# Retention attention, routing and experts in one kernel: the attention's products put in another order on TensorE

## The chip, the cores and the metric

The kernel runs on one core of a Trainium2 chip. The metric is the time of one execution on the device, in microseconds (us), as the median of several executions. The engines are PE (TensorE, the matmuls; PEld is its weight load), DVE (VectorE), ACT (ScalarE), POOL (GpSimd) and SP (SyncE, which here issues most transfers). Each has its own instruction stream, which it works through in order.

## The reference

Three layers follow one another, all in float32. In the attention, each head keeps a state that decays by a fixed factor at every position; eight heads of 64, two batches of 768 positions:

```python
for t in range(S):
    state = gamma * state + einsum('bhd,bhe->bhde', k[:, :, t], v[:, :, t])
    y[:, :, t] = scale * einsum('bhd,bhde->bhe', q[:, :, t], state)
x = y as 1536 rows of 512
# experts: two of eight per row, by noisy logits
noisy = x @ w_gate + log1p(exp(x @ w_noise)) * noise
top2, weights = the two largest, softmax over the two
out[rows of e] += weight * (relu(x[rows of e] @ w1[e]) @ w2[e])
# last layer
h = out @ w_in;  solu = h * softmax(h)
out = layer_norm(solu) * g_ln @ w_out
```

## The kernel before

**Tiles.** The attention works on 12 tiles of 128 positions: six chunks c of each of two batches b, in the order (c, b). The heads stand in pairs. For tile i these are the steps; the lines are those of the kernel before.

- `scores(i)`: 8 matmuls that use half of the array's rows each (L432) write queries times keys into a bank; DVE multiplies by the causal mask (L436). The result is PM(i).
- `y_out(i)`: 4 matmuls on the full array bring queries times state ("state(i)", L445; none for the first chunk), and 8 on half of the array's columns add PM(i) times the scaled values ("values(i)", L449), into the one bank `c2`. DVE copies this, scaled, to XT(i) (L452) and so frees the bank.
- `kv(i)`: 4 matmuls on the full array add keys times values to the state ("keys(i)", L460; none in the last chunk). ACT copies the result to S (L466).
- `x_rows(i)`: 4 matmuls on the full array turn XT(i) into rows, with the routing's logits beside them (L482). ACT copies the two halves to x (L485, L487), DVE copies the logits to lgs and adds the second half (L486, L488), SP stores x.
- `scale_v(i)`: the values scaled by the decay, vp(i), on DVE for i < 5 and from there in 8 instructions on ACT (L422). `dec_t` makes the decay tables decT in 4 instructions on ACT (L301).
- `feed`: loads units of the experts' weights (wr, L182, SP) and splits each into a high part wh on ACT (L200) and a low part wl on DVE (L201). The wl of a unit waits in the list `later` and is written down at the next tile's place for it.

In fp32r, the form that the experts' matmuls use, a value is a sum of two parts; hence `wh`, `wl` and `xh`, `xl`.

**Routing.** It goes by four groups of tiles, g = 0 to 3, of 4, 4, 2 and 2 tiles. `choose(g)` is a generator: two functions on ACT (L504, L505), a chain of 11 small instructions on DVE (L507 to L513), then the two largest logits, `chosen` and `cum` (L517 to L520), then their indices (L523). `rank(g)` counts on PE (L533), with ACT's copy rks (L534); `first_rows(g)` makes `s` (L544) and compares `col`, the column numbers, with it to a one-hot `oh` (L548). `list_part` multiplies `oh` on PE (L607, L613) to lists of rows (L619), by which POOL gathers rows of x (L622); `first_xt` transposes these (L635) for the first expert. `slots`, `add_table` and `by_rows` (L565 to L601) make the table of places. `hidden(0, f)` is the first expert's first layer (L724).

**What sets the order.** One loop over i, written by hand, sets the order of all these on each engine. Before the change, tile i runs state(i) and values(i), then keys(i), then scores(i+1), then x(i), and the routing's pieces stand between by conditions on i. PE changes between half rows, half columns and the full array four times per tile from the third tile on. The first expert's weights follow: `feed` loads the units (whose number is `LEAD` and a few) during the tiles. After the attention come the experts 0 to 7, which PE paces, then the last layer and the stores (L958, L959).

## Time and profile before

| what | value |
|---|---|
| three executions | 517.97, 518.2, 519.29 us; median 518.2 |
| the profiled execution | 519.29 us |
| its span in the profile | 517.6 us |
| PE clock granted | 0.999 |
| PE, PEld, DVE, ACT, POOL busy | 98, 89, 71, 45, 19% |

The profile is of one execution. Its span goes from the first to the last recorded instruction; the execution's own time is 1.7 us longer. A busy share is an average over stages that have different limits: the attention is the first 72 us of the span, the experts and the last layer the rest.

### The profile page before, as it was taken

Reading aid. Unit: us, or ns where it says so; the run is one execution under the profiler, and the core shown is the slowest. Engines: PE = TensorE matmul, PEld = TensorE weight load, DVE = VectorE, ACT = ScalarE, POOL = GpSimd, SP = SyncE. Lnnn points to the kernel's source line nnn. Section 1 sums busy time; section 2 is a strip of 40 time slices with the busy share of each in tenths; the row PEclk is TensorE's granted clock in tenths of the full one; section 3 lists DMA queues with packets and bytes.
Section 4 is the critical chain, followed back from the end, with each engine's and each line's share of the span. In section 5 each row is a group of like instructions: output and inputs, shape, how many; then the busy total and the mean of one; then the engine's idle time right before and its main releaser. Section 6 shows DMA issues by size and latency. Waiting matters only on the chain.

```text
span 517.6 us, 8642 instructions
## 1 busy us (share of the span) xinstructions
PE 506.3 (98%) x3068; PEld 462.9 (89%) x3068; DVE 370.1 (71%) x750; ACT 233.5 (45%) x435; POOL 98.4 (19%) x202
## 2 busy tenths in 40 slices
PE   8999999999999999999999999999999999999996
PEld 7888888989999999999999999998878788888886
DVE  4769888747776976878778778799277668566650
ACT  2487642544344443344435443445254544444431
POOL 4000011431201203103003000002244346411120
PEclk9999999999999999999999999999999999999999
DMA  8999531498999988979999967567553565653341
GB/s 253 310 403 317 194 114 42 145 318 277 292 309 267 292 249 215 335 209 262 319 236 315 290 203 240 192 182 211 158 187 89 176 184 142 204 142 103 101 123 46
DMA packets 71857, 111.92 MB, mean 216 GB/s; under 512 B 9760, under 2 KB 37152, under 8 KB 71808
## 3 DMA queue, kind: packets, MB, share of 16 engines
q1 hardware_dynamic: 65520, 94.58, 60.5%
q0 software_dynamic: 4944, 16.39, 9.7%
q8 instruction: 26, 0.43, 0.3%
q10 hardware_dynamic: 1344, 0.34, 0.3%
q14 instruction: 23, 0.19, 0.1%
HBM read 83.50 MB, written 27.79 MB: 215 GB/s over the span
## 4 chain that ended last, share of the span: by engine, by line
PE 74%; DVE 13%; issue 6%; DMA 3%; ACT 2%; POOL 0%; SPq 0%; POOLq 0%; DVEq 0%; ACTq 0%
PE c L1068 18%; PE b L952 12%; PE b L724 11%; PE a L724 10%; PE d L865 10%; PE c L1190 3%; PE s L432 2%; DVE wl L201 2%; PE c L449 2%; DMA wr<-in_moe_w_dram 2%; PE c L460 1%; DVE pm L436 1%; PE c L445 1%; DVE rt L510 1%; PE c L482 1%
## 5 line engine op out<-in xcount | busy, mean ns | idle before, releaser
L201 DVE TENSOR_TENSOR wl<-wr,wh 128x1024 fp32r<-128x1024 f32 x68 | 81.5, 1218 | 14.5 <-issue 7.8
L1068 PE MATMUL c<-hh,wh 128*128 128x448 f32 (+5 forms) x224 | 78.9, 352 | 0.0
L1068 PE MATMUL c<-hh,wl 128*128 128x448 f32 (+5 forms) x224 | 78.8, 352 | 0.0
L1068 PE MATMUL c<-hl,wh 128*128 128x448 f32 (+5 forms) x224 | 78.8, 352 | 0.0
L200 ACT ACTIVATE wh<-wr 128x1024 fp32r<-128x1024 f32 x68 | 69.5, 1049 | 8.7 <-DMA wr<-in_moe_w_dram 8.7
L724 PE MATMUL b<-xh,wh 128*128 128x192 f32 (+8 forms) x144 | 47.1, 335 | 0.3 <-ACT xh L639 0.3
L724 PE MATMUL b<-xh,wl 128*128 128x192 f32 (+8 forms) x144 | 46.6, 331 | 0.0
L1068 PEld LDWEIGHTS c<-hh,wh 128*128 128x128 f32 x224 | 42.1, 188 | 1.1
L1068 PEld LDWEIGHTS c<-hh,wl 128*128 128x128 f32 x224 | 42.0, 188 | 1.1
L1068 PEld LDWEIGHTS c<-hl,wh 128*128 128x128 f32 x224 | 42.1, 188 | 1.1
L724 PE MATMUL a<-xh,wh 128*128 128x256 f32 (+7 forms) x128 | 43.0, 340 | 0.0
L724 PE MATMUL a<-xh,wl 128*128 128x256 f32 (+7 forms) x128 | 42.8, 339 | 0.0
L952 PE MATMUL b<-wh,zh 128*128 128x512 f32 (+1 forms) x104 | 38.5, 376 | 0.6 <-ACT zh L941 0.6
L865 PE MATMUL d<-wh,x2h 128*128 128x512 f32 x96 | 38.8, 404 | 0.0
L952 PE MATMUL b<-wl,zh 128*128 128x512 f32 (+1 forms) x104 | 38.4, 375 | 0.0
L865 PE MATMUL d<-wl,x2h 128*128 128x512 f32 x96 | 37.9, 395 | 0.0
L865 PE MATMUL d<-wh,x2l 128*128 128x512 f32 x96 | 37.8, 394 | 0.0
L728 ACT ACTIVATE hh<-b 128x192 fp32r<-128x192 f32 (+8 forms) x36 | 17.1, 476 | 43.6 <-PE b L724 40.6
L728 ACT ACTIVATE hh<-a 128x256 fp32r<-128x256 f32 (+7 forms) x32 | 15.9, 497 | 45.3 <-PE a L724 45.3
L1105 POOL COPY pace<-hh 1x1 f32<-1x1 f32 x20 | 8.7, 437 | 133.3 <-ACT hh L728 79.1
L1031 ACT ACTIVATE xh<-xt 128x428 fp32r<-128x428 f32 (+5 forms) x24 | 13.0, 540 | 44.8 <-DVE xt L1029 44.8
L878 ACT ACTIVATE ee<-d,st 128x1024 f32<-128x1024 f32 x12 | 13.4, 1117 | 41.7 <-DVE st L871 41.7
(259 smaller groups left out, 1100.4 us busy)
## 6 DMA issues: line engine op xcount, KB each, us to landing
wr<-in_moe_w_dram SPq DMA_DIRECT2D x60, 512.0 KB
zd<-zs SPq DMA_DIRECT2D x40, 128.0 KB
zc<-zd SPq DMA_DIRECT2D x10, 512.0 KB
xs<-xr SPq DMA_DIRECT2D x18, 256.0 KB
raw<-in_moe_w_in_dram SPq DMA_DIRECT2D x8, 512.0 KB
raw<-in_moe_w_out_dram SPq DMA_DIRECT2D x8, 512.0 KB
xq<-xs SPq DMA_DIRECT2D x16, 208.0 KB
yg<-yr SPq DMA_DIRECT2D x16, 208.0 KB
```

What stands on the lines that cost most here:

```text
L200: nc.scalar.activation(hi, t, AF.Copy)
L201: low = lambda: nc.vector.tensor_sub(lo, t, hi)
L432: nc.tensor.matmul(p[:, s, hp, :], KT[i][r, hp, :], QT[i][r, hp, :], start=True, stop=True)
L449: nc.tensor.matmul(py[s * 64:s * 64 + 64, hp, :], VP[i][:, 2 * hp + s, :], PM[i][hp // 2][:, hp % 2, s, :], start=(not c), stop=True, skip ...
L724: nc.tensor.matmul(p, w[:, 0, f * 128:(f + 1) * 128], x[:, d, c], start=(n == 0), stop=(n == len(terms) - 1))
L728: nc.scalar.activation(hh[:, f, c], p, AF.Relu)
L865: nc.tensor.matmul(PH[i][:, s, :], x[:, c], w[:, 0, f], start=(n == 0), stop=(n == 3 * KD - 1))
L878: nc.scalar.activation(ee, ph, AF.Exp, bias=col(0), accum_out=col(1))
L952: nc.tensor.matmul(p, z[:, f * 128:(f + 1) * 128], unit_t[8 * E + 4 + f // 2][n][:, f % 2, c], start=(m == 0), stop=(m == len(terms) - 1))
L1031: nc.scalar.activation(hi, t, AF.Copy)
L1068: nc.tensor.matmul(py[d][:, :CAPS[e]], c, h[:, f, :CAPS[e]], start=(f == 0 and n == 0), stop=(f == KF - 1 and n == 2))
L1190: nc.tensor.matmul(py, h[:, f, c], w[:, f % 2], start=(f == 0 and n == 0), stop=(f == KF - 1 and n == 2))
```

## The change

Keys(i), state(i) and x(i-1), all on the full array, now stand together, then values(i), then scores(i+1). `y_out` is cut into `from_state` and `y_out`. The routing's pieces move with this to other places in the loop; rank(2) and first_rows(2) move from the end of the attention to behind the first `hidden(0, 0)`. The column numbers `col` become F16. `feed` splits the first unit one tile earlier and loads the third and the fourth one tile later, and low parts that wait in `later` are not written down at tile 4. The second half of the last store is issued by ACT. Lines of the new kernel stand 4 higher from L453 on.

```diff
-    col = rt.tile([128, CAPS[0]], F32, name="col", bufs=1)
+    col = rt.tile([128, CAPS[0]], F16, name="col", bufs=1)
...
-    def y_out(i):
+    def from_state(i):
         c, b = order[i]
-        py = bank("c2", (128, HP, 128))
+        py = PO[i] = bank("c2", (128, HP, 128))
         if c:
             for hp in range(HP):
                 nc.tensor.matmul(py[:, hp, :], S_bufs[b, c % 2][:, hp, :], QT[i][:, hp, :],
                                  start=(hp == 0), stop=False, skip_group_check=True)
+
+    def y_out(i):
+        c, b = order[i]
+        py = PO.pop(i)
...
     for i in range(NT):
         load_qk(i + 3)
         load_kv(i + 3)
-        if i == 0:
-            kv(i)
+        kv(i)
+        from_state(i)
+        if i:
+            x_rows(i - 1)
+        if i == 6:
+            rank(0)
+            next(picks, None)
+        if i == 10:
+            list_part(0, range(4, 8), "a", last=True)
+            next(picks, None)
+        if i in (4, 8, 10):
+            picks = choose((4, 8, 10).index(i))
+            next(picks)
         y_out(i)
-        if i in (5, 8, 11):
+        if i in (5, 8):
             next(picks)
         if i == 7:
             next(todo, None)
-        if i:
-            kv(i)
+        if i == NT - 1:
+            for d in (0, 2):
+                first_xt(0, d, f"c{d // 2}")
+            next(picks)
+        scores(i + 1)
+        if i in (4, 8, 10):
+            next(picks)
         if i == 8:
             add_table(0)
             by_rows()
         if i == 9:
             rank(1)
             first_rows(1)
-        if i == NT - 1:
-            for d in (0, 2):
-                first_xt(0, d, f"c{d // 2}")
-            rank(2)
-        scores(i + 1)
-        if i in (4, 8, 10):
-            next(picks)
-        if i == 9:
-            next(picks, None)
...
-        for low in later:
-            low()
-        later = []
+        if i != 4:
+            for low in later:
+                low()
+            later = []
...
-        x_rows(i)
-        if i == 5:
-            rank(0)
-            next(picks, None)
-        if i == 9:
-            list_part(0, range(4, 8), "a", last=True)
-        if i in (3, 7, 9, 11):
-            if i == NT - 1:
-                last_picks = picks
-            picks = choose((3, 7, 9, 11).index(i))
-            next(picks)
         scale_v(i + 2)
         if i % 2 == 0:
             dec_t(i // 2 + 1)
-        feed(min(max(i - 2, 0), LEAD), min(i, LEAD + 3), later)
-    next(picks)
-    next(picks)
-    first_rows(2)
-    guard(EARLY_TILES)
+        feed((0, 0, 1, 1, 2, 3)[i] if i < 6 else LEAD, (0, 1, 2, 2, 3)[i] if i < 5 else min(i, LEAD + 3), later)
+    x_rows(NT - 1)
+    last_picks = picks
+    picks = choose(3)
+    for _ in range(3):
+        next(picks)
...
-        nc.sync.dma_start(out[row0(i):row0(i) + 128, c], o[:, c])
+        (nc.scalar if c.stop == DM and c.start else nc.sync).dma_start(out[row0(i):row0(i) + 128, c], o[:, c])
...
-    def newest():
-        rank(3)
-        first_rows(3)
+    def newest(g):
+        rank(g)
+        first_rows(g)
+        if g == 2:
+            guard(EARLY_TILES)
...
-        hidden(0, f, slice(0, EARLY), newest if f == 2 else None)
+        hidden(0, f, slice(0, EARLY), (lambda: newest(2 + f // 2)) if f in (0, 2) else None)
```

The instruction lists of both kernels show three places. A row has the line, the operation, the tile written and those read, and the shape; numbers behind a name tell buffers apart.

On PE, tile 4 before, from x(3), which writes `c_535`, to x(4), which writes `c_619`:

```order
L482 MATMUL c_535<-unit_166,xT 128x144 x2
L482 MATMUL a<-unit_167,xT 128x144 x2
L445 MATMUL c_572<-qt,S_227 128x128 x4
L449 MATMUL c_572<-pm,vp 64x128 x8
L460 MATMUL c_254<-vp,kn 128x128 x4
L432 MATMUL s<-qt,kt 128x128 x8
L482 MATMUL c_619<-unit_166,xT 128x144 x2
L482 MATMUL a<-unit_167,xT 128x144 x2
```

The same place after, from values(3) to scores(5):

```order
L453 MATMUL c_498<-pm,vp 64x128 x8
L432 MATMUL s<-qt,kt 128x128 x8
L464 MATMUL c_254<-vp,kn 128x128 x4
L445 MATMUL c_562<-qt,S_227 128x128 x4
L486 MATMUL c_567<-unit_166,xT 128x144 x2
L486 MATMUL a<-unit_167,xT 128x144 x2
L453 MATMUL c_562<-pm,vp 64x128 x8
L432 MATMUL s<-qt,kt 128x128 x8
```

Here x(3), which is `c_567`, moved from ahead of state(4) to behind it, keys(4) moved from behind values(4) to ahead of state(4), and scores(5) follow the values at once.

On ACT, before, from the state copy of tile 4 (`S_229`) to that of tile 5 (`S_233`); x<-c_619 is x(4):

```order
L466 ACTIVATE S_229<-c_254 64x4x64 x2
L485 ACTIVATE x<-c_619 128x256
L487 ACTIVATE x<-a 128x256
L422 ACTIVATE vp<-vt,dec 128x64 x8
L301 ACTIVATE decT<-decT,step 128x128 x4
L200 ACTIVATE wh<-wr 128x1024
L466 ACTIVATE S_233<-c_255 64x4x64 x2
```

After, from the same state copy; x<-c_567 is x(3) and x<-c_655 is x(4):

```order
L470 ACTIVATE S_229<-c_254 64x4x64 x2
L489 ACTIVATE x<-c_567 128x256
L491 ACTIVATE x<-a 128x256
L508 ACTIVATE rt<-lgs 128x32
L509 ACTIVATE rt<-lgs 128x32
L422 ACTIVATE vp<-vt,dec 128x64 x8
L301 ACTIVATE decT<-decT,step 128x128 x4
L200 ACTIVATE wh<-wr 128x1024
L470 ACTIVATE S_233<-c_255 64x4x64 x2
L489 ACTIVATE x<-c_655 128x256
L491 ACTIVATE x<-a 128x256
```

x(4) stood ahead of the scaled values vp(6), the decay table and wh, and now stands behind them.

On DVE, before, from the logits of x(8) to XT(10), which reads `c_1088`:

```order
L486 COPY lgs<-c_970 128x16
L488 TENSOR_TENSOR lgs<-lgs,a 128x16
L452 TENSOR_TENSOR xT<-c_996,decT 128x512
L544 SCALAR_TENSOR_TENSOR s_1021<-chosen,rks 128x4
L548 TENSOR_SCALAR oh<-col,s_1021 128x448 x4
L436 TENSOR_TENSOR pm<-s,causal 128x512 x2
L523 MAX_INDEX ix<-top,rt 128x8 x4
L524 CAST top_i<-ix 128x8
L486 COPY lgs<-c_1049 128x16
L488 TENSOR_TENSOR lgs<-lgs,a 128x16
L619 TENSOR_SCALAR rows_186<-a 96x2
L452 TENSOR_TENSOR xT<-c_1088,decT 128x512
```

After, the same stretch; XT(9) reads `c_990`, XT(10) `c_1053`:

```order
L490 COPY lgs<-c_995 128x16
L492 TENSOR_TENSOR lgs<-lgs,a 128x16
L456 TENSOR_TENSOR xT<-c_990,decT 128x512
L436 TENSOR_TENSOR pm<-s,causal 128x512 x2
L548 SCALAR_TENSOR_TENSOR s_1034<-chosen,rks 128x4
L552 TENSOR_SCALAR oh<-col,s_1034 128x448 x4
L490 COPY lgs<-c_1058 128x16
L492 TENSOR_TENSOR lgs<-lgs,a 128x16
L623 TENSOR_SCALAR rows_186<-a 96x2
L527 MAX_INDEX ix<-top,rt 128x8 x4
L528 CAST top_i<-ix 128x8
L456 TENSOR_TENSOR xT<-c_1053,decT 128x512
```

PM(10), which is the `pm` row, moved ahead of `s` and the four compares, and the indices (MAX_INDEX) moved behind the row lists.

## Rows read from the trace of the kernel before

**Rows 1.** Section 1 of the page: busy us, share of the span, instructions.

```profile
PE 506.3 (98%) x3068; PEld 462.9 (89%) x3068; DVE 370.1 (71%) x750; ACT 233.5 (45%) x435; POOL 98.4 (19%) x202
```

**Rows 2.** Busy time by engine in 40 to 50 us (start:end, sum, then each engine).

```profile
40.00:50.00 10.00, 10.00 (x110) 9.05 (x110) 9.35 (x31) 8.90 (x29) 0.00 (x0) 1.00 0.90 301
```

**Rows 3.** Timeline of PE in one tile (start us, busy us, engine, line, operation).

```profile
26.83 0.65 PE L482 MATMUL a<-unit,xT 128*128 128x144 f32 x4
27.32 1.05 PE L445 MATMUL c<-qt,S 128*128 128x128 f32 x8
28.30 1.09 PE L449 MATMUL c<-pm,vp 128*64 128x128 f32 x16
29.33 1.16 PE L460 MATMUL c<-vp,kn 128*128 128x128 f32 x8
30.42 1.16 PE L432 MATMUL s<-qt,kt 64*128 64x128 f32 x16
```

**Rows 4.** Timeline of PE in tile 10: list_part, then values, scores and x.

```profile
61.55 0.81 PE L613 MATMUL a<-number,oh 128*96 128x1 f16 x8
...
63.29 1.09 PE L449 MATMUL c<-pm,vp 128*64 128x128 f32 x16
64.32 1.16 PE L432 MATMUL s<-qt,kt 64*128 64x128 f32 x16
65.41 0.39 PE L482 MATMUL c<-unit,xT 128*128 128x144 f32 x1
```

**Rows 5.** Timeline of PE at three waits, whose idle time stands in brackets.

```profile
11.34 0.36 PE L482 MATMUL c<-unit,xT 128*128 128x144 f32 x1 [0.52 <-DVE xT L452]
...
37.80 0.48 PE L482 MATMUL c<-unit,xT 128*128 128x144 f32 x2 [0.95 <-DVE xT L452]
...
70.86 0.37 PE L482 MATMUL c<-unit,xT 128*128 128x144 f32 x1
```

**Rows 6.** Timeline of DVE, 31 to 70 us.

```profile
31.63 1.29 DVE L436 TENSOR_TENSOR pm<-s,causal 128x512 f32<-128x512 f32 x2 [1.49 <-PE s L432]
...
35.48 1.22 DVE L201 TENSOR_TENSOR wl<-wr,wh 128x1024 fp32r<-128x1024 f32 x1
...
43.30 1.29 DVE L436 TENSOR_TENSOR pm<-s,causal 128x512 f32<-128x512 f32 x2 [0.24 <-PE s L432]
...
58.94 0.68 DVE L452 TENSOR_TENSOR xT<-c,decT 128x512 f32<-128x512 f32 x1
60.32 0.16 DVE L544 SCALAR_TENSOR_TENSOR s<-chosen,rks 128x4 f32<-128x4 bf16 x1 [0.70 <-ACT rks L534]
60.52 1.54 DVE L548 TENSOR_SCALAR oh<-col,s 128x448 f16<-128x448 f32 x4
...
66.73 0.17 DVE L507 SCALAR_TENSOR_TENSOR rt<-rt 128x16 f32<-128x16 f32 x1
...
69.19 0.17 DVE L486 COPY lgs<-c 128x16 f32<-128x16 f32 x1
...
69.54 0.68 DVE L452 TENSOR_TENSOR xT<-c,decT 128x512 f32<-128x512 f32 x1
```

**Rows 7.** The one-hot compare of line 548, its two widths (all eight, ns).

```profile
L548 DVE TENSOR_SCALAR oh<-col,s x8: 348/400/453, 60.5 to 78.1; 128x448 f16<-128x448 f32 x4, 128x256 f16<-128x256 f32 x4
```

**Rows 8.** Timeline of ACT in one tile.

```profile
33.08 2.01 ACT L422 ACTIVATE vp<-vt,dec 128x64 f32<-128x64 f32 x8
...
36.15 1.05 ACT L200 ACTIVATE wh<-wr 128x1024 fp32r<-128x1024 f32 x1
37.10 0.76 ACT L466 ACTIVATE S<-c 64x256 f32<-64x256 f32 x2
```

**Rows 9.** Timeline: a load's issue on SP, its first use on DVE, a weight unit's issue.

```profile
5.16 0.43 SPq L250 DMA_DIRECT2D vt<-in_v_dram  x1
...
9.90 0.69 DVE L419 TENSOR_TENSOR vp<-vt,dec 128x512 f32<-128x512 f32 x1 [2.34 <-DMA vt<-in_v_dram]
...
18.97 0.33 SPq L182 DMA_DIRECT2D wr<-in_moe_w_dram  x1
```

More of the change, by code (lines that the diff above doesn't have):

```diff
@@ L410, in retnet_moe_solu @@
     pS = [bank(f"c{b}", (128, HP, 128)) for b in range(B)]
-    VP, PM, XT = {}, {}, {}
+    VP, PM, XT, PO = {}, {}, {}, {}
     def scale_v(i):
```

## Prediction

> **What bounds the kernel now.** I read the page first. PE is busy 98% of the span and its weight loads 89% [rows 1], so PE looks like the bound everywhere. A busy PE is not a PE at its peak, though, and the change lies wholly in the first 90 us, so I read that stretch by itself. There, between 40 and 50 us, DVE is busy 9.35 us of 10 and ACT 8.90 [rows 2]. These three engines hand work round in a ring: scores on PE give PM on DVE, PM gives the values on PE, these give XT on DVE, and XT frees the one bank `c2` for the next tile's state product. Then I read PE's timeline for the price of a switch between ways of using the array. Matmuls that follow their own kind run at 0.49 us for x's second half, 4 of 144 columns, so 0.87 us for 8 of 128 (0.49 / 4 x 8 x 128/144). The keys' product, which stands between two products of other forms, takes 29.33 to 30.42, 1.09 [rows 3]. One block has one switch into it and one out of it, each shared with a neighbour, so one switch is about 0.2 us. Last I read which PE waits stand in this stretch [rows 5] and what DVE does before them [rows 6].
>
> The Trainium skill (Perfetto Trace Analysis, Identifying the Most-Contended Engine) says the same of the 98%: matmul occupancy is no measure of the distance to the roofline, weight-load busy is a better one; here that is the 89%.
>
> **The change on PE.** A tile had four switches and has three in tiles 1 to 9; tiles 0, 10 and 11 keep their number. That is 9 x 0.2 = 1.8 us of PE time. It is not saved if the third switch, now straight from the column-split values to the row-split scores, is dearer than the two it replaces. Tile 10 of the trace before has exactly that neighbourhood: values 63.29 to 64.32, 1.03, and scores to 65.41, 1.09 [rows 4], just what they take in a tile with the keys between (1.03 and 1.09, [rows 3]). So 1.8 us of PE time does go. What it is worth depends on the ring, and I follow it in four stretches up to x_rows(11), behind which the weights, lists and gathers are paced by PE and any gain is kept. The edits and their stretches:
>
> **A, to PM(5), which starts at 31.63.** The x product of tile 0 waited 0.52 for XT(0) (11.34, [rows 5]); now tile 1's keys stand before it. With the four or five switches saved by then, PE could be about 1.4 us earlier: 0.5 and 0.9. But the split of weight unit 0 (ACT wh, 0.95) is moved one tile ahead, and on ACT it now stands before tile 3's S copies and the copies of x(2). The load is issued at 18.97 before [rows 9], some 0.6 earlier after. A value load took 4.74 from issue (5.16) to the first use that waited for it (9.90, [rows 9]); the unit is 256 KB larger, which is 0.85 at the 301 GB/s of [rows 2]. So it lands at about 18.4 + 4.7 + 0.8 = 23.9. This is an estimate; its bounds are 23.1 (size counts nothing) and 27.9 (time doubles with size). Behind it come wh 1.0, the S pair 0.75 [rows 8], x(2)'s two copies of the same width, 0.65, and on DVE the lgs pair 0.35 and XT(3) 0.6 [rows 6], all in order, and only then is bank c2 free: state(4) at about 27.2, against 27.32 before [rows 3]. So PE waits there about 1.3 us, and of the 1.4 some 0.1 is left; the new order puts x(3) behind that state and saves one more switch, so PM(5) starts 0.1 to 0.5 earlier. I take **0.3**.
>
> **B, PM(5) to the end of XT(9), 31.63 to 59.54 [rows 6].** DVE is the bound here. The wl of unit 0 (35.48, busy 1.22, 1.1 between starts) leaves the tile with the first poly chain and is done ahead of PM(5), where DVE was idle for 1.49 (31.63): a gain of 1.1. The one idle time for scores, 0.24 at 43.30, goes too, since PE is then ahead. The PE waits before x(5) (37.80, 0.95, [rows 5]) and before values(9) were for this DVE, so removing them is no gain of its own. Against it: lgs(i-1) now stands in DVE's order straight ahead of XT(i) and waits for ACT's copies of x(i-1), which on ACT stand behind vp(i+2), decT and wh: 33.08 to 36.15 for the first two and to 37.10 with wh, 4.0 us [rows 8], where before x(4) stood ahead of them. If ACT starts vp(6) at about 31.6, after x(3) and the routing's first two functions, the queue and a further S pair, 4.0 and 0.75, bring x(4) to 37.0; DVE, through PM(5) and the chain, is there at about 36.1. So DVE waits about 0.9 for x(4). For x(6), with the same queue ahead of it but DVE further behind because of `slots`, I get between 0 and 0.4. The net gain is 1.1 + 0.2 - 0.9 = 0.4, less 0 to 0.4; if x(4) holds DVE only half as long it is 0.8. I take **0.4**, since DVE is behind at x(6). XT(9) then ends near 58.8.
>
> **C, XT(9) to x_rows(11), 59.54 to 70.86 [rows 5, 6]: 11.32 before.** Before, DVE waited 0.70 for rks, did `s` and the compares, then PM(10); PE did state(10) behind list_part. After, the path is: PM(10) 1.2, `s` 0.2, four compares, list_part behind the last of them, values(10) 1.03, scores(11) 1.09 and 0.1 to reach DVE, PM(11) 1.2, the poly chain 2.45 (66.73 to 69.19), lgs 0.35 (to 69.54), XT(11) 0.6 [rows 4, 6]. list_part took 0.81 whole with waits among them [rows 4]; behind the last compare half of it is left, 0.35 with the trip. The compares are the unknown: an F16 `col` in place of F32. They take 0.36 each now: 1.54 for four, less the last one's whole 0.45, over three. All eight go from 348 ns at 256 columns to 453 at 448 [rows 7], so 0.55 ns a column and about 0.2 us that is not columns. No row shows a 16-bit source for this operation. Bounds: nothing, and all of the column part, 0.245 each. I take half of it, 0.115 each, since the result was 16-bit already: four of 0.25 are 1.0. The sum is 1.2 + 0.2 + 1.0 + 0.35 + 1.03 + 1.09 + 0.1 + 1.2 + 2.45 + 0.35 + 0.6 = 9.57. The gain is 11.32 - 9.57 = **1.7**, between 1.3 (F16 nothing) and 2.2 (column part gone). What pays it: the idle 0.70 for rks, because rank(1) now runs while PM(10) does; state(10), 1.0, which now runs beside the compares; the four compares; rank(2), which left the place before x_rows(11). It pays for PM(10), 1.2, which has moved onto this path.
>
> The Trainium skill (VectorE: DVE Perf Modes, Mode 4×_2P — both tricks at once) gives a single-source operation four 16-bit elements a cycle where 32-bit ones get two. By it the column part would halve; the sum would be the same.
>
> **D, from x_rows(11) on.** Chain(3) on DVE stays the path, now with rank(2) and first_rows(2) behind hidden(0,0): four compares of 256 columns save 0.06 each by half the slope, and rank(2)'s wait for DVE can come back behind hidden. I take 0, between -0.3 and +0.3. The later units' loads and gathers follow PE's pace. The last store's second half goes out from ACT's queue: an issue takes 0.33 on SP [rows 9], so it is worth at most that either way; I take 0.
>
> **Sum.** 0.3 + 0.4 + 1.7 + 0 = 2.4 us. The profiled execution took 519.29 and becomes 516.9; it is the slowest of the three before. From the median, 518.2, I get **515.8**. About 0.3% (1.55 us) is what a measurement of this kernel can tell from no change, by the spread of these three runs.
>
> **Rivals.**
> - *PE alone.* If DVE's and ACT's backlog hides (unit 0 lands at 23.1 or before, the x copies are there in time), all 1.8 of the switches count, and beside them the waits of [rows 5], 0.52 + 0.95, and half of C's 1.7, the part that is DVE's: about 4.1, so 514.1. For it speaks that PE was 98% busy; against it the 9.35 of DVE. 0.19.
> - *The ring gives it back.* ACT's x copies come later than I think (1.4 and 0.5 of wait in B, so B loses 0.6 where I have +0.4) and F16 changes nothing (C 1.3). The gain is 0.3 - 0.6 + 1.3 = 1.0: 517.2. To it belongs that the change does not do what it says, a dearer third switch; [rows 4] speak against that. 0.23.
> - *Slower: ACT held by a weight unit's landing.* ACT works in order, so wh(0) holds S, x, vp behind it till unit 0 is there. Each us of landing after 23.9 is a us of state(4), then of PM(5) and all behind it. From 26.3 on the gain is gone; at the bound of 27.9, a load that takes twice a value's time, 4.0 - 2.4 = 1.6 are lost: 519.8. For it speaks that the load shares the queues with keys, queries and values; against it that a value load came in 4.74. 0.08.
> - My forecast: 0.50, its own range 514.9 to 516.6.
>
> The range goes from 514.0, at the PE-alone case, to 517.6, over most of the give-back. Faster is my forecast and PE alone, 0.69; same 0.23; slower 0.08.
>
> **What would show it.** PE: keys, state and x in one run, a tile 0.2 shorter; values and scores still 1.03 and 1.09. The waits at 11.34 and 37.80 gone. In their place: state(4) idle 1.1 to 1.5, released by XT(3), with ACT's wh(0) idle before it on the DMA of wr; DVE's lgs(4) idle about 0.9 on ACT's x; state(10) idle near 0.9 on XT(9); list_part on the last compare 0.4; x_rows(11) on XT(11). XT(9) ends near 58.8; x_rows(11) starts near 68.4. Compares of 448 columns 0.25 apart. Behind 90 us the trace should be the old one, 2.4 us earlier. Wrong it would be if F16 left the compares at 0.36, if state(4) did not wait (A is then 1.3 more) or waited over 3 us, or if the x copies did not hold DVE.

## The result, and the profile after

The changed kernel is slower: median 523.39 us (522.11 to 524.96, six executions) against 518.53 us (517.97 to 519.32, six) for the kernel before; ratio 1.0089, interval 1.0072 to 1.0107. 515.8 was predicted. The profiled execution took 523.6 us, its span is 522.0, and the mean granted clock of its six executions is 0.987 to 0.994.

The same matmuls in the two traces show where the time goes (starts in us, and the end of the span from the trace to 0.01 us; the step is what is added since the row above):

| matmul | before | after | difference | step |
|---|---|---|---|---|
| x_rows(11) | 70.86 | 70.66 | -0.20 | -0.20 |
| a matmul of expert 0 | 88.58 | 91.08 | +2.50 | +2.70 |
| first transposition of the next rows (L1025, L1029) | 115.39 | 117.45 | +2.06 | -0.44 |
| a matmul of an expert's first layer | 206.26 | 209.70 | +3.44 | +1.38 |
| last matmul | 513.04 | 516.27 | +3.23 | -0.21 |
| end of the span | 517.65 | 521.96 | +4.31 | +1.08 |

Section 1 of the page after, and PE's clock in 40 slices of 13 us (answers to [rows 1]):

```profile
span 522.0 us, 8621 instructions
PE 509.3 (98%) x3068; PEld 465.6 (89%) x3068; DVE 369.8 (71%) x750; ACT 233.1 (45%) x435; POOL 99.1 (19%) x202
PEclk9999979999999999999999999999999999999998
```

The instructions are the same and PE is "98%" again, yet it is busy 3.0 us longer. One slice has a lower clock, the sixth, and the windows show when: columns are sum, then PE, PEld, DVE, ACT and POOL busy, PE's clock, DMA share, GB/s.

```profile
60.00:70.00 10.00, 8.62 (x98) 7.69 (x98) 7.54 (x37) 3.95 (x14) 2.10 (x2) 1.00 0.29 94
70.00:72.00 2.00, 1.34 (x10) 1.37 (x10) 1.93 (x7) 0.38 (x1) 0.00 (x0) 0.91 0.04 8
72.00:78.00 6.00, 6.00 (x31) 5.96 (x31) 4.50 (x27) 1.45 (x6) 0.00 (x0) 0.50 0.45 132
78.00:80.00 2.00, 2.00 (x19) 1.99 (x18) 0.43 (x4) 0.41 (x2) 0.00 (x0) 0.89 0.00 0
80.00:90.00 10.00, 9.23 (x91) 8.58 (x89) 8.91 (x40) 2.74 (x7) 1.92 (x2) 1.00 0.19 55
```

PE's timeline shows what it did before: scores(11) at 63.46, state, x(10), values(11), first_xt, and then 2.04 us of nothing.

```profile
63.46 1.16 PE L432 MATMUL s<-qt,kt 64*128 64x128 f32 x16
64.55 1.16 PE L445 MATMUL c<-qt,S 128*128 128x128 f32 x8
...
67.74 0.88 PE L639 MATMUL c<-unit,xr 96*128 96x96 f32 x8
70.66 0.73 PE L486 MATMUL c<-unit,xT 128*128 128x144 f32 x4 [2.04 <-DVE xT L456]
...
72.16 0.41 PE L728 MATMUL b<-xh,wh 128*128 128x192 f32 x1
72.38 0.41 PE L728 MATMUL b<-xh,wl 128*128 128x192 f32 x1
...
84.30 0.28 PE L728 MATMUL b<-xh,wl 128*128 128x192 f32 x1
```

Before, [rows 5], x_rows(11) had no wait of its own: first_xt and rank(2) stood ahead of it, with waits of 0.73 and 0.30 us between. Now PE is idle, and from 71.6 us, 0.9 us after this wait ended, the granted clock is 0.50 for 6.8 us, the level of 1.2 GHz: matmuls of 192 columns start 0.21 us apart, at full clock 0.11. That is the +2.70. The Trainium skill (TensorE: Matmul & The Clock Gate, What's actually happening) says that the clock is held back by default and activity releases it; the fall behind an idle PE agrees, though the same wait came without a fall in another execution (after_again, below).

DVE's timeline shows what PE waited for:

```profile
59.13 0.68 DVE L456 TENSOR_TENSOR xT<-c,decT 128x512 f32<-128x512 f32 x1
61.12 1.08 DVE L552 TENSOR_SCALAR oh<-col,s 128x448 f16<-128x448 f16 x4
65.81 1.29 DVE L436 TENSOR_TENSOR pm<-s,causal 128x512 f32<-128x512 f32 x2 [1.51 <-PE s L432]
69.83 0.68 DVE L456 TENSOR_TENSOR xT<-c,decT 128x512 f32<-128x512 f32 x1
```

The last matmul of scores(11) starts at 64.35, and PM(11) 1.46 us later, with DVE idle. In the trace before that step is 0.32 (65.21 to 65.53), and DVE is idle for 0.40:

```profile
65.53 1.29 DVE L436 TENSOR_TENSOR pm<-s,causal 128x512 f32<-128x512 f32 x2 [0.40 <-PE s L432]
```

PE had gone on to state(11) at 64.55, so the product was all but done; what came late is its signal to DVE, whose record in the trace stands at 65.78. POOL's timeline has something in just that time:

```profile
63.00 1.17 POOL L626 DMA_INDIRECT xr<-xd,rows  x1 [54.93 <-DVE rows L623]
64.47 0.93 POOL L626 DMA_INDIRECT xr<-xd,rows  x1 [0.30 <-issue]
```

The second gather's issue runs from 64.47 to 65.40, and PM(11) starts 0.41 behind it. Before, these issues stood at 64.73 and 66.20.

The two last steps of the table: between 117 and 206 us the experts' matmuls of 448 columns start 207 ns apart and not 203; and the span ends 4.85 us behind the end of the last ACT copy and not 3.77.

```profile
516.63 0.47 ACT L960 ACTIVATE o<-b,st 128x256 f32<-128x256 f32 x1 [2.25 <-PE b L954]
```

The theories. **T1**: a PE that is left idle loses its clock (+2.7), and the idle time is long because PM(11)'s signal is late beside POOL's second issue (+1.1). **T2**, a rival: ACT's new last store makes the end later, or more. **T3**, a rival: `feed`'s new times hold ACT and so the ring. **T4**, a rival: what is late at PM(11) is PE's own neighbourhood, the state product straight behind the scores.

### The profile page after: what moved, and what is told of

Its sections match the earlier page's. It is cut to its first block, busy times and chain, and to the rows that moved or that the text cites. A ratio compares the mean times of both kernels' runs of the same rounds, so it can differ in the third digit from the quotient of the medians.

```text
span 522.0 us, 8621 instructions
## 1 busy us (share of the span) xinstructions
PE 509.3 (98%) x3068; PEld 465.6 (89%) x3068; DVE 369.8 (71%) x750; ACT 233.1 (45%) x435; POOL 99.1 (19%) x202
## 4 chain that ended last, share of the span: by engine, by line
PE 72%; DVE 13%; issue 6%; ACT 4%; DMA 3%; POOL 1%; SPq 0%; POOLq 0%; DVEq 0%; ACTq 0%
PE c L1072 18%; PE b L954 12%; PE b L728 11%; PE a L728 10%; PE d L867 10%; PE c L1194 3%; DMA wr<-in_moe_w_dram 3%; DVE wl L201 2%; PE s L432 1%; DVE pm L436 1%; ACT wh L200 1%; PE c L464 1%; DVE xT L456 1%; PE c L728 1%; PE c L453 1%
## 5 line engine op out<-in xcount | busy, mean ns | idle before, releaser
L728 PE MATMUL b<-xh,wh 128*128 128x192 f32 (+8 forms) x144 | 48.6, 343 | 0.2 <-ACT xh L643 0.2
L728 PE MATMUL b<-xh,wl 128*128 128x192 f32 (+8 forms) x144 | 48.0, 339 | 0.0
```

The lines of the kernel that those rows point to most:

```text
L728: nc.tensor.matmul(p, w[:, 0, f * 128:(f + 1) * 128], x[:, d, c], start=(n == 0), stop=(n == len(terms) - 1))
```

## The experiments

Each was timed beside runs of the kernel before on the same chip. All but one start from the changed kernel. The fillings and the longer warm-up are matmuls whose result nobody uses. The ratio is estimated over all executions and is not the quotient of the two medians.

| run | median us | before | ratio | interval |
|---|---|---|---|---|
| store_sp | 519.51 | 518.58 | 1.0008 | 0.9995 to 1.0021 |
| fill | 517.51 | 518.58 | 0.9975 | 0.9964 to 0.9986 |
| swap11 | 519.24 | 518.58 | 1.0008 | 0.9993 to 1.0024 |
| feed_as_before | 518.62 | 518.58 | 1.0003 | 0.9988 to 1.0017 |
| after_again | 521.01 | 518.94 | 1.0049 | 1.0028 to 1.0071 |
| fill_sp | 518.37 | 518.94 | 0.9996 | 0.9979 to 1.0014 |
| chain_late | 525.06 | 518.94 | 1.0108 | 1.0084 to 1.0132 |
| col_f32 | 522.42 | 518.94 | 1.0078 | 1.0060 to 1.0096 |
| swap_fill | 518.52 | 518.80 | 0.9993 | 0.9978 to 1.0009 |
| gather_shift | 518.00 | 518.80 | 0.9991 | 0.9973 to 1.0009 |
| fill_again | 518.10 | 518.80 | 0.9992 | 0.9976 to 1.0008 |
| before_store | 518.39 | 518.80 | 0.9993 | 0.9980 to 1.0007 |
| gs_again | 519.31 | 518.89 | 1.0007 | 0.9991 to 1.0022 |
| gs_feed | 519.42 | 518.89 | 1.0005 | 0.9992 to 1.0018 |
| gs_late | 519.75 | 518.89 | 1.0016 | 1.0000 to 1.0033 |
| warm10 | 516.74 | 519.46 | 0.9949 | 0.9932 to 0.9966 |
| gs_feed_warm10 | 517.55 | 519.46 | 0.9965 | 0.9952 to 0.9978 |
| gs_warm10 | 516.67 | 519.04 | 0.9959 | 0.9945 to 0.9974 |

**First chip: the store, the idle PE, the order, the feed.**

store_sp undoes the store:

```diff
-        (nc.scalar if c.stop == DM and c.start else nc.sync).dma_start(out[row0(i):row0(i) + 128, c], o[:, c])
+        nc.sync.dma_start(out[row0(i):row0(i) + 128, c], o[:, c])
```

> The changed kernel with the last store's second half issued by SP again, all else as changed. In the profile of the changed kernel the last ACT copy starts at 516.63 and the span ends at 522.0, 5.4 later; before it was 513.41 and 517.6, 4.2 later, while PE's last matmuls stand 3.40 apart. Theory: the ACT issue costs 1.0 to 1.2 at the very end. Then the last copy and the end of the span are 4.2 apart here and the median falls by about 1.1, to 522.3. Rival: the end is later for another reason (the store's own transfer); then they stay 5.4 apart and the time stays at 523.4.

The end stays long: 4.93 us from the last copy, 4.85 in after. T2 falls. But, against both expectations, 3.9 us of the loss are gone all the same, and not by the store (before_store, below): on this chip PM(11) starts 0.32 after the scores' last matmul begins, in the same order and beside the same POOL issue, and x_rows(11) waits 0.99, not 2.04, without a fall of the clock there.

fill gives PE something to do until XT(11) is there (bf16 ones, behind first_xt in tile 11):

```diff
+            fill = bank("s", (128, 128))
+            for n in range(34):
+                nc.tensor.matmul(fill, ones, ones, start=True, stop=True)
```

> The changed kernel with 34 extra bf16 matmuls of 128 columns into the idle bank s, behind first_xt of tile 11 and ahead of x_rows(11): extra work that no result uses. Theory: the 2.04 us in which PE stood idle ahead of x_rows(11) made the granted clock fall to 0.5 from 71.8 to 78.2 us, and this cost 2.8 us. Then with the gap filled the clock stays at 1.0 there and the median falls by 2.5 to 3.3, to about 520.5. Rival: the first hidden products are slow because of rank(2) and the compares that now stand behind hidden(0,0); then the fill changes nothing or adds up to 0.5: 523.4 to 523.9, and the clock falls all the same.

Faster than before, and the clock is at least 0.998 in all twelve executions. PE and the windows, 70 to 80 us:

```profile
68.16 2.06 PE L779 MATMUL s<-ones 128*128 128x128 bf16 x34
70.06 0.71 PE L486 MATMUL c<-unit,xT 128*128 128x144 f32 x4
```

```profile
70.00:80.00 10.00, 9.99 (x105) 9.85 (x102) 8.06 (x50) 2.90 (x11) 1.43 (x2) 1.00 0.28 84
```

Its end took only 3.54 us, which no theory had foretold, so not all of the gain is the clock's.

swap11 puts x(10) ahead of state(11), so that scores(11) have another neighbour:

```diff
+        if i == NT - 1:
+            x_rows(i - 1)
         from_state(i)
-        if i:
+        if i and i < NT - 1:
             x_rows(i - 1)
```

> The changed kernel with x(10) ahead of state(11) in tile 11 alone. There scores(11) was followed at once by state(11), and PM(11) saw scores(11) 1.44 us after its last matmul began, where all other tiles show 0.30. Theory: it is the state product directly behind the scores that holds the signal; then PM(11) starts about 0.3 after the scores' last matmul, x_rows(11) starts 1.1 earlier, the idle time ahead of it falls from 2.04 to about 0.9, and if the clock holds the median falls by 1.1 + 2.8 = 3.9, to 519.5; if it falls all the same, by 1.1. Rival: the late signal came by chance in one execution; then it is at 0.30 in this run whatever the order, or late again.

It tells nothing: the signal was prompt here in any order.

feed_as_before restores the old call of `feed` and writes low parts down at tile 4 too:

```diff
-        if i != 4:
-            for low in later:
-                low()
-            later = []
+        for low in later:
+            low()
+        later = []
...
-        feed((0, 0, 1, 1, 2, 3)[i] if i < 6 else LEAD, (0, 1, 2, 2, 3)[i] if i < 5 else min(i, LEAD + 3), later)
+        feed(min(max(i - 2, 0), LEAD), min(i, LEAD + 3), later)
```

> The changed kernel with the weight units loaded, split and flushed as in the kernel before (unit 0 split at tile 3, its wl in the tile of the first poly chain). Theory of the prediction: wh(0) ahead of tile 3's copies holds state(4) by its load; without that state(4) no longer waits (0.34 idle at 27.30), PM(5) starts up to 1 us earlier than 31.61, and wl back in the chain's tile costs 1.1 of DVE; XT(9) ends within 0.5 of 59.73 and the time stays within 1 us of 523.4. Rival: the split's early place is what cost A its gain; then XT(9) ends over 0.8 earlier, near 58.9.

The time is not near the 523.4 that was expected; the signal is prompt on this chip. It is not faster than store_sp beyond the intervals, and PM(5) is at 32.29, XT(9) at 59.29, inside what the new feed gives on this chip (31.18 to 33.37, 58.47 to 59.53). What holds ACT in tile 5 is a value load here too, so T3 falls as a cause of the loss:

```profile
27.24 2.02 ACT L422 ACTIVATE vp<-vt,dec 128x64 f32<-128x64 f32 x8 [3.95 <-DMA vt<-in_v_dram]
```

**Second chip: is the late signal there, and what is each part worth?**

after_again is the changed kernel once more.

> The changed kernel, unchanged. In its first profile PM(11) was signalled 1.44 us after the scores' last matmul began, x_rows(11) waited 2.04 us and the clock fell to 0.5; in four kernels that differ from it little the signal came at 0.30, the wait was 1.0 or filled, and the clock stayed at 1.0. Theory one, a chance event of those executions: then this run has the signal at 0.30, a wait of 1.0 ahead of x_rows(11), x_rows(11) about 1.1 earlier than 70.66, and a median of 518 to 519.5. Theory two, a property of the kernel as built: then the signal is late again, the clock falls, and the median is 523 again.

The late signal is back (1.55) and so is the wait. Its median loss is 2.1 us, not 4.9, and its profile has the wait without the fall:

```profile
70.36 0.73 PE L486 MATMUL c<-unit,xT 128*128 128x144 f32 x4 [2.04 <-DVE xT L456]
```

```profile
72.00:78.00 6.00, 5.99 (x68) 5.81 (x67) 4.98 (x30) 1.81 (x8) 0.00 (x0) 1.00 0.43 132
```

So the two profiles of one kernel price the clock: from x_rows(11) to the same matmul of expert 0 it takes 20.42 us in after and 17.53 here, 2.89 less. The clock of its nine executions is 0.987 to 0.998: the same wait costs the clock in some executions and not in others.

fill_sp is fill and store_sp together.

> The changed kernel with both single edits that were tried, the 34 extra matmuls ahead of x_rows(11) and the last store from SP. If the store from ACT costs 1 us at the end, the median is 1 us below the 517.5 of the fill alone, 516.5; if it costs nothing, 517.5.

The signal is late (1.55), but PE is fed: 2.6 us faster than after_again on the same chip, clock 0.996 to 1.0. The end accounts for 1.2 of it (3.77 against 4.96); that the rest is the clock's is argued from the granted clocks.

chain_late moves the chain of group 2 on DVE behind XT(11), so that XT(11) comes earlier, and ranks and first rows of groups 2 and 3 one `hidden` later:

```diff
                 first_xt(0, d, f"c{d // 2}")
             next(picks)
+            next(picks)
         scores(i + 1)
-        if i in (4, 8, 10):
+        if i in (4, 8):
             next(picks)
...
-        hidden(0, f, slice(0, EARLY), (lambda: newest(2 + f // 2)) if f in (0, 2) else None)
+        hidden(0, f, slice(0, EARLY), (lambda: newest(2 + f // 2)) if f in (1, 3) else None)
```

> The changed kernel with the poly chain of group 2 behind XT(11) and the transposes' low parts instead of ahead of them, and rank(2), rank(3) behind hidden(0,1) and hidden(0,3) instead of (0,0) and (0,2). Theory: the wait ahead of x_rows(11) is the DVE chain (2.45 us) in front of XT(11); without it x_rows(11) follows the transposes with under 0.3 us of wait, nothing lets the clock fall, and the chain's time comes back only in part, behind the hidden products: the median is 1 to 2 us under the 518.5 of the kernel before. Rival: DVE is the bound all the way, the wait moves whole to rank(2) and rank(3), and the time is that of the kernel before within 0.5.

The wait moved and did not go. x_rows(11) starts at 67.90 and waits 0.07, but then counting and lists wait in turn, and the clock falls there, from 77.4 for 10.2 us:

```profile
76.08 0.18 PE L537 MATMUL a<-chosen,before 128*128 128x16 bf16 x1 [0.94 <-DVE chosen L522]
...
77.52 0.41 PE L617 MATMUL c<-number,oh 128*128 128x1 f16 x4 [0.67 <-DVE oh L552]
...
78.70 0.41 PE L617 MATMUL c<-number,oh 128*128 128x1 f16 x4 [0.77 <-DVE oh L552]
```

```profile
78.00:87.00 9.00, 8.30 (x42) 8.20 (x43) 6.60 (x32) 0.66 (x2) 1.91 (x2) 0.50 0.19 58
```

It is the slowest of all, with x_rows(11) 3 us earlier than before: the clearest sign that the start of x_rows(11) does not decide. No single wait in this stretch is longer than 0.94.

col_f32 gives `col` its old type:

```diff
-    col = rt.tile([128, CAPS[0]], F16, name="col", bufs=1)
+    col = rt.tile([128, CAPS[0]], F32, name="col", bufs=1)
```

> The changed kernel with the column numbers in F32 again. The prediction took the four compares at 0.25 each with F16 against 0.36 with F32; the profile of the changed kernel has 1.08 for the four. Expected: 1.54 for the four, list_part and all behind it up to x_rows(11) 0.45 later than with F16. Rival: DVE is not on the path there, and values(10) start at the same distance behind XT(9).

```profile
60.69 1.54 DVE L552 TENSOR_SCALAR oh<-col,s 128x448 f16<-128x448 f32 x4
```

1.54 against 1.08: F16 saves 0.46 on the four compares, and 0.43 from XT(9) to x_rows(11) (11.44 against 11.01 in after_again).

**Third chip: what makes the signal late?**

swap_fill is swap11 and fill together.

> The changed kernel with x(10) ahead of state(11) in tile 11 and the 34 extra matmuls of the fill ahead of x_rows(11), extra work that no result uses. In five profiles of kernels with state(11) directly behind scores(11), PM(11) was signalled 1.2 us later than in four others, one of which had x(10) in between. Theory one, the neighbourhood: here the signal is at 0.30 after the scores' last matmul, and with the idle time filled the median is 0.2 to 0.3% below the kernel before. Theory two, the gather that POOL issues at that moment: then the order on PE changes nothing, and the signal is late if this execution is of the kind that shows it.

PM(11) comes 1.44 after the scores, with x(10) and not the state behind them. T4 falls. Nor is it DVE alone that is told late: ACT's copy of x(10) starts 1.35 us after x(10) on PE, and 0.84 in swap11, where the signal was prompt (64.94 to 65.78). In the trace the signals of the scores and of the two halves of x(10) all come between 65.03 and 65.15, 0.06 apart, though the matmuls that give them start between 63.61 and 64.77.

```profile
63.81 0.76 PE L486 MATMUL c<-unit,xT 128*128 128x144 f32 x4
65.16 0.38 ACT L489 ACTIVATE x<-c 128x256 f32<-128x256 f32 x1 [2.91 <-issue]
```

gather_shift moves the indices of group 1 ahead of the list, so that POOL issues later and its first gather's issue, not the second, falls on the signal:

```diff
         if i == 10:
+            next(picks, None)
             list_part(0, range(4, 8), "a", last=True)
-            next(picks, None)
```

> The changed kernel with the indices of group 1 (0.73 us of DVE) ahead of the row lists of tile 10, so that POOL's two gather issues come 0.7 us later; PE's order is that of the changed kernel. In the profiles with the late signal it came 0.38 to 0.47 after the end of POOL's second issue. Theory, POOL: PM(11)'s signal moves with POOL's issues, to prompt (0.30) or later by 0.7. Rival, PE's neighbourhood: the signal is 1.44 to 1.52 after the scores' last matmul began, whatever POOL does. If the signal is prompt in this run and in the other kernels of this job alike, nothing is told.

The issues start at 64.73 and 66.20, the last matmul of scores(11) at 65.31, and the signal takes 0.32; in swap_fill and fill_again, on the same chip, it takes 1.44 and 1.43. So PE's neighbourhood is out, and the lateness goes with POOL's second issue; but that is one trace against two, and whether it is the issue or the first gather's transfer, which runs beside it (3.3 us from issue to landing in gs_feed), no run tells. The gain did not show in the median: in the profile, state(4) waits for its bank, and the clock is down for 3.4 us there, long before the place in question.

```profile
28.25 1.01 PE L445 MATMUL c<-qt,S 128*128 128x128 f32 x3 [2.39 <-DVE xT L456]
```

fill_again is fill on this chip.

> The changed kernel with the fill, unchanged against its first run. If what it gained there, 0.25% against the kernel before, holds, the median is again 0.8 to 1.5 us below it; if that was bound to executions in which the signal to PM(11) is prompt, and this one shows it late, the gain is 1.1 less and the ratio is 1.000 within 0.002. In both cases the granted clock stays at 1.0 behind 70 us.

The signal is late again (1.43). The interval overlaps that of fill, so what a late signal costs a PE that is fed isn't told by the two.

before_store is the kernel before with the last store on ACT.

> The kernel before with the last store's second half issued by ACT, and nothing else of the change. Theory: it is worth nothing measurable, since the store lands 1.7 to 2.0 us after its issue from either queue; the median is that of the kernel before within 0.4. Rival, from the first profile of the changed kernel: the end of the program comes 1.2 us later behind a store from ACT; then the median is 1.0 to 1.2 higher.

No difference in the median, and its end takes 3.54: the store does not make it long. It even shortens it a little: of the nine short ends the seven with the last store from ACT take 3.54 or 3.55, the two with it from SP (before, fill_sp) 3.77.

**Fourth chip: gather_shift with three feeds.** gs_again repeats it; gs_feed adds feed_as_before; gs_late adds a feed one tile later:

```diff
+        feed(min(max(i - 3, 0), LEAD), min(max(i - 1, 0), LEAD + 3), later)
```

> The changed kernel with the indices ahead of the row lists, as in gather_shift, for a firmer time. POOL theory: PM(11) is signalled at 0.30 again, the wait ahead of x_rows(11) stays under 1.0, and the median is 0.1 to 0.3% under the kernel before, with single executions 1.5 to 2 higher where the clock fell behind a long wait of state(4). Rival: the prompt signal of gather_shift was chance; then it is late again, x_rows(11) waits 2.0 and the median is 521.

> As gs_again, with the weight units loaded and split as in the kernel before. If unit 0's early split is what costs stretch A its gain, state(4) no longer waits and XT(9) starts 0.5 to 1.0 earlier than in gs_again; if the values' loads hold ACT as well (in feed_as_before ACT waited 3.95 for vp(5)'s values), state(5) waits in its place, XT(9) starts within 0.5 of gs_again and the medians are the same within 0.5.

> As gs_again, with the first unit loaded at tile 2 and split at tile 4, one tile later than in the kernel before, so that fewer loads run beside those of the values. Theory, the loads compete: ACT waits less than 0.5 for values in tiles 3 to 5, state(4) and state(5) do not wait, PM(5) starts near 30.5, a low part of 1.1 comes back to DVE between there and XT(9), which starts near 58.0, and the median is 1.5 to 2.5 us under the kernel before. Rival: the transfers are at their limit anyway (395 GB/s from 20 to 40 us) and values come late without the units; then PM(5) starts near 31.5 and the low part makes XT(9) later than in gs_again by up to 1.1.

All three have the prompt signal (0.32), XT(9) to x_rows(11) in 9.78 or 9.79, and no gain, where the theories for gs_again and gs_late had foretold one. gs_feed's XT(9) starts 1.19 earlier than gs_again's (state(4) waited 1.48 there and not at all in gs_feed), and yet the medians are the same. gs_feed's last matmul starts at 510.97, 2.07 us earlier than before, but its end takes 5.44, 1.67 more. gs_late has PM(5) early, at 30.37, and loses it where wl now stands ahead of XT(9):

```profile
59.85 1.16 PE L445 MATMUL c<-qt,S 128*128 128x128 f32 x8 [1.93 <-DVE xT L456]
```

What stood between these kernels and their gain was the end, as far as the profiles show: the last matmuls start 0.65 to 2.07 earlier than before, and the ends take 1.60 to 1.71 more. In the traces so far, the ends of 4.84 to 5.48 us are all those of the changed order without a filling, 3.54 to 3.77 those of the kernel before and of the fillings. PE's list has 6,189 records in the changed kernel (3068 matmuls, as many weight loads, 53 others) and 6,201 in the one before, whose only surplus is twelve semaphore instructions.

The traces also hold the control instructions by which the engines wait for one another at the very end, and they show where the time stands. In ten of the eleven traces with a long end, PE is released with the other engines (in after at 520.06) and starts its next instruction 1.5 to 2.3 us later (521.73), though it waits for nothing that the trace shows; in the nine others that step is 0.1 (517.06 to 517.15 before). The late instruction is record 6,188 of PE's list in each. swap11's list is one record longer, and there it is again record 6,188 that is late, now the wait itself (516.84, against 514.97 on the other engines). In the longer lists that record is a matmul or a weight load of the last layer, and none is late there. So, as far as these traces go, what parts the two is where the list ends, and not its length as such. The next three runs move that end, by matmuls at the very start.

**Fifth and sixth chip: ten more warm-up matmuls.** warm10 has them alone, the others on gs_feed and gather_shift:

```diff
-    for n in range(34):
+    for n in range(44):
```

> The changed kernel with ten more of the 34 warm-up matmuls that stand at the start and that no result uses; PE waits there for the first keys, so they cost at most 0.6. Theory: the end of the program depends on the length of PE's instruction list, and the end behind the last copy falls from 4.9 to about 3.6; the median is 1.0 to 1.3 lower than the changed kernel's in the same kind of execution (520 against 521 to 523, as the clock falls or not). Rival: the end depends on what the last store or the fill's place does; then it stays at 4.8 to 5.5.

> gs_feed with the ten more warm-up matmuls: the prompt signal, the feed of the kernel before and the longer list together. gs_feed's profile had its last matmul 2.1 us earlier than the kernel before and its end 1.7 longer. Theory: with the end at 3.6 the median is 1.2 to 1.9 us under the kernel before, 0.25 to 0.35%. Rival: the end is chance; then the median is that of the kernel before within 0.6, as gs_feed's was.

> The changed kernel with the indices ahead of the row lists and ten more warm-up matmuls. Theory: the signal is prompt in either kind of execution, x_rows(11) waits under 1.0, the end is 3.6 behind the last copy, and the median is 1.5 to 2.8 us under the kernel before (0.3 to 0.5%), with single executions 1.5 to 2 later where state(4) waited long and the clock fell. Rival: the gain of warm10 was its execution's alone; then the median is that of the kernel before within 0.8.

All three beat the kernel before. Their ends are 3.55 each, though what was added stands 500 us ahead of the end. gs_feed_warm10 gains less, and its profile is one with 207 ns. warm10 lies 3.3 us under the 520 foretold, which did not reckon with a prompt signal and a clock of 0.998 or more in all its executions. With the signal prompt, it can't show whether the shift is needed; gs_warm10 has both and is the version to keep. Its page, DVE and PE:

```profile
span 514.7 us, 8641 instructions
```

```profile
58.35 0.68 DVE L456 TENSOR_TENSOR xT<-c,decT 128x512 f32<-128x512 f32 x1
...
63.88 1.29 DVE L436 TENSOR_TENSOR pm<-s,causal 128x512 f32<-128x512 f32 x2 [0.40 <-issue]
```

```profile
62.67 1.16 PE L432 MATMUL s<-qt,kt 64*128 64x128 f32 x16
...
67.61 0.80 PE L639 MATMUL c<-unit,xr 96*128 96x96 f32 x7 [0.45 <-DMA xr<-xd,rows]
68.73 0.73 PE L486 MATMUL c<-unit,xT 128*128 128x144 f32 x4 [0.32 <-ACT xh L643]
```

PE's long wait has become two of 0.45 and 0.32, x_rows(11) starts 2.13 earlier than before [rows 5], the last matmul 2.68 (510.36 against 513.04), and the clock is 0.997 or more in all twelve executions. The same ten matmuls in the kernel before weren't tried; its end already took 3.77, so little of the gain can come from there, but that is argued and not shown.

Of T1, then, the clock's part is shown: one kernel with and without the fall, and none in the fillings' profiles. The late signal's part is measured, 2.04 of wait for 0.99, and its link to POOL's second issue rests on the third chip. The rest of the loss that T2 looked for is at PE's end of list.

## Why the prediction was wrong

**The step that failed is D**, "I take 0, between -0.3 and +0.3", with "behind 90 us the trace should be the old one". A PE wait was priced at its own length, so that the wait of x_rows(11) for XT(11) was to cost nothing beyond its start, and a clock that falls behind it had no term; nor had the end. From x_rows(11) on the profiled execution lost 4.5 us: 2.70 by the clock, 1.38 by the pace, 1.08 at the end, less 0.44 and 0.21. fill_sp against after_again shows that feeding PE brings back the clock's share and the end's together; warm10 shows the end's without a filling. The pace is not shown to belong to the change: after_again is the same kernel and runs at 203 ns.

**A** (0.3 predicted, 0.02 measured). Unit 0 landed as worked out, wh(0) starts at 24.04 for 23.9, and state(4) at 27.30 for 27.2. But PE was not 1.4 us early by then: tile 0's scores took 0.8 longer than before, scores(4) start 0.42 earlier (24.72 for 25.14), and state(4) waits 0.34, not 1.3. From state(4) to PM(5) it takes 4.31 in both traces, since x(3), 1.07, stands where keys(4), 1.09, stood: the further switch gave nothing there. The values landed late, which had no term, and held lgs(3) on DVE, so that XT(4) ends no earlier than the scores. PM(5) starts at 31.61 for 31.63 [rows 6]. PE, DVE and ACT:

```profile
4.93 2.03 PE L432 MATMUL s<-qt,kt 64*128 64x128 f32 x16
...
27.30 1.16 PE L445 MATMUL c<-qt,S 128*128 128x128 f32 x8 [0.34 <-DVE xT L456]
...
30.55 0.17 DVE L490 COPY lgs<-c 128x16 f32<-128x16 f32 x1 [0.97 <-ACT x L489]
...
37.12 0.17 DVE L490 COPY lgs<-c 128x16 f32<-128x16 f32 x1 [1.57 <-ACT x L489]
...
24.04 1.06 ACT L200 ACTIVATE wh<-wr 128x1024 fp32r<-128x1024 f32 x1 [3.77 <-DMA wr<-in_moe_w_dram]
...
27.41 2.02 ACT L422 ACTIVATE vp<-vt,dec 128x64 f32<-128x64 f32 x8 [0.98 <-DMA vt<-in_v_dram]
...
36.70 0.38 ACT L489 ACTIVATE x<-c 128x256 f32<-128x256 f32 x1
```

**B** (0.4 predicted, -0.2 measured). x(4) on ACT starts at 36.70 for 37.0, and DVE waits for it 1.57, not 0.9. The mis-sized term is DVE's arrival, taken as 36.1: by [rows 6] PM(5) and the chain take 3.85 (31.63 to 35.48), and DVE was there at 35.55. So the 1.1 of the low part was more than spent, and some 0.3 came back at PM(7). XT(9) starts at 59.13, 0.19 later than before, where 58.2 or so was worked out. The gain of A and B is within what varies anyway: XT(9) starts between 57.93 and 60.18 in the traces of the changed order.

**C** (9.57 predicted, for 11.32). 10.93 after, and 9.77 to 9.79 in each of ten traces with the prompt signal and no filling: the sum was right to 0.2, which is the step from XT(11) to x_rows(11), 0.83 for 0.6. What was mis-sized here is one term, "0.1 to reach DVE", which was 1.26 (64.55 to 65.81). F16's 0.115 a compare was right (0.46 for four). By the Trainium skill (VectorE: DVE Perf Modes, Mode 4×_2P — both tricks at once) the column part halves, and the traces agree: from 256 to 448 columns a compare grows by some 50 ns with F16 (281 to 332) and some 100 with F32 (348 to 448).

**The rivals.** The change did what it says: a tile takes 5.08 us from scores to scores (14.56, 19.64, 24.72) where it took about 5.27. The slower rival's unit load came in time (24.04, and 26.3 was the point from which it decides). So the slower side was reached by a way that no rival named. With the clock, the signal and the end out of the way, gs_warm10 gains 2.4 us, the 2.4 of the sum. That the two agree is in part luck: its trace has 0.59 up to XT(9), 1.54 from there to x_rows(11) and 0.55 behind, where 0.7, 1.7 and 0 were predicted, and XT(9) alone moves by 2.2 between traces.

**Open.** Why the signal is late only on some chips: with the same issue beside it, it took 0.32 on the first and the fifth. What PE does ahead of its record 6,188, when that is one of its last three (the place fits all twenty traces; the cause of the halt no row shows). Why some executions fall in clock behind a wait and others not. Why four of the twenty traces have 207 ns and not 203. How much of the median's loss of 4.9 is the chip's: on the second the same kernel lost 2.1.

## What to carry to other kernels

A wait moved onto PE is priced by what PE does before and after it: if the new order leaves PE idle, ask for the clock behind it, and give it something to do or leave work between (before, the transposes and rank(2) cut the idle time into 0.73 and 0.30). Read a reordering's gain at two places, where the stretch ends and at the last instruction, since here 0.2 us gained at the one was 4.3 lost at the other. And see what other engines issue just when a signal on the path is due.

## What was not expected of the hardware

- A signal from PE to DVE took 1.43 to 1.55 us (0.32 otherwise, from the start of the last matmul) where it was due while POOL issued the second of two gathers, in seven traces (the first result's, the second and the third chip's); in five others it was prompt beside the same issue (store_sp: due at 64.0, second issue 63.81 to 64.74), and during the first issue it was prompt in every trace (gs_warm10: due at 63.9, first issue 62.97 to 64.14). In swap_fill PE's signals to ACT were held back with it.
- From the last copy to the end of the span it took 4.84 to 5.48 us in eleven traces and 3.54 to 3.77 in nine. The queue of the last store does not part them. In the eleven, PE halts ahead of its record 6,188, which is there among its closing control instructions (1.67 us in after, 0.09 at that step before), and ten matmuls at the start move the list's end away from it.
- One idle time of 2.04 us was followed by a clock of 0.50 for 6.8 us in one execution (after) and of 1.00 in two others (after_again; col_f32 with 2.05).
